# GpSimd and VectorE by turns in the planner, weight scans as squares on ScalarE, v split in two operations, two more second layers in sevens

## The chip, the cores and the metric

One core of one Trainium2 chip. The metric is device time in microseconds (us) for one execution. Engines are named as in the profile: PE is TensorE's matmul and PEld its weight load, DVE is VectorE, ACT is ScalarE, POOL is GpSimd, SP is SyncE, which here issues every DMA.

## What is computed

The reference is block-sparse attention followed by a mixture of four experts that takes all of them for every token:

```
scores_l = scale * q @ k.T            (only |i - j| < 16 kept)
scores_s = scale * q @ max_of_32(k) + log(32)
a = softmax(concat(scores_l, scores_s))
x = a @ concat(v, mean_of_32(v))      -> 3072 tokens x 512
for e in range(4):
    h = relu(x @ w1[e])               (512 -> 1024)
    out += p[:, e:e+1] * (h @ w2[e])  (1024 -> 512)
```

with 4 batches, 8 heads, 768 positions, 64 channels a head; p is `domain_probs` divided by its sum over the experts. Everything comes in and goes out as fp32.

## The kernel before, in words

**Precision.** Each fp32 matmul is done as three matmuls in a narrower type: an operand is split into a high part (a cast, on ACT) and a low part (the difference, on POOL or DVE), and hi x hi, hi x lo and lo x hi are summed in PSUM. For fp16 parts the weights are scaled to use the type's range. The scale of an expert's two matrices comes from `largest` (line 425), a maximum of absolute values on DVE for each 128 x 512 piece of a weight, collected in `wmax`, and from `scales_of_weights` (line 455), which turns the 128 partial maxima through PE, takes their maximum and makes a power of two and its inverse out of it in a chain of small DVE operations. `scan` (line 468) loads one piece (tile `ws`) and calls `largest`; there are 4 experts x 8 pieces x 2 matrices = 64 of them, in the order of experts 2, 3, 1, 0.

**Stages.** The first 768 tokens are done by `plain_units`, two blocks of 384 with experts 0 and 1 in fp32r; the profile's names there are ph, po<-w. Then follow the four pairs of blocks in `PAIRS` (line 1264), each with its list of experts: pair 0 has experts 2 and 3, pair 1 has 3, 2, 1, 0, pair 2 has 0, 1, 2, 3 and pair 3 has 3, 2, 1, 0. For pairs, the first layer (`first`, line 1516) is a 2 x 2 block product with seven instead of eight products (the table `SEVEN`; PSUM tiles pha to phd). The combined operands of x are made once for each pair by `x_operands`, those of w1 once for each expert by `w1_operands` (tiles `w1g`, kept in DRAM and loaded again by later pairs).

**The second layer** has two forms. The plain form is `mm2`, called by `second` and `tile_by_tile` (po<-w2s,h, 512 columns): for each of six tiles of 128 tokens eight slices of the hidden units with three matmuls each. Its weights come from `w2_scaled` (line 1104; tiles `w2s`, stored once and loaded by later pairs), and it is interleaved with the first layer of the next expert. The other form is `second_sevens` (line 1415; poa to pod, 256 columns): the same 2 x 2 scheme with seven products. Its weights come from `w2_operands` (line 1193; tiles `w2g`), which loads two raw pieces, scales them on ACT, makes four casts on ACT, four combinations on DVE and four low parts, one half on POOL and the other on the engine that is passed as `low`. Its hidden units are combined and split by `h_operands` (line 1474). `SEVENS` (line 1265) lists the pairs and experts that use this form: experts 0, 1, 2 of pair 2 and all of pair 3. `fetch7` (line 1297) prepares the next entry of `todo7` during a second layer, `fetch2` the next of `todo2`, which holds the plain ones.

**Attention** runs in between as 64 pieces of 96 queries x 4 heads: `load_piece`, `stage_a` (line 608: splits k, q and v), `scores`, `probs`, `transposed`, `values`, `to_x`. From the second batch on, `stage_a` scales v on ACT, casts it on ACT and subtracts on POOL.

**The order.** No engine call is issued at once. Each becomes a `Step` (line 87) with a cost from a formula for its engine (`takes`, how long the engine is held, and `lasts`, when the result is there). `order_of` (line 164) then runs a list scheduler over the whole program: `forward` (line 298) places ready steps by rank on the five engines, with buffers given out in order of first use; `backward` (line 321) does the same from the end and gives new ranks. Ten rounds are made and the best order kept, and the kernel is issued in that order. The constants stand at lines 65 to 67: `WAIT` (signalling between engines), `SPARE` (a tenth added to the cost of every step on ACT, DVE and POOL) and `ROUNDS`.

## Time and profile before

| | |
|---|---|
| time, median of 3 runs | 1079.7 us (1079.17 to 1083.99) |
| profiled execution | 1079.39 us, span 1077.5 us, mean granted clock 0.995 |
| instructions | 22082 |
| DMA | 194.95 MB, 181 GB/s over the span |
| stages, by the time of their matmuls | plain blocks up to 207 us, pair 0 to about 352, pair 1 to about 606, pair 2 to about 850, pair 3 to the end |

[...] A group of instructions is written out<-in with the tile names above. A wait is listed as who waited, for whose result. "PE 98% busy" counts matmuls from start to modelled end, so the pitch of matmuls in a clean run is the better price.

### The profile page before, as it was taken

How to read it: one execution, taken by the hardware profiler on the slowest of the kernel's cores; microseconds unless marked ns; L12 is line 12 of the kernel's file. 1: busy time of each engine (PE TensorE's matmuls, PEld its weight loads, DVE VectorE, ACT ScalarE, POOL GpSimd, SP SyncE). 2: the span in 40 equal slices, each digit the busy share in tenths (PEclk: the TensorE clock that was granted, in tenths of full speed). 3: DMA queues.
4: the chain of work that ended last, by engine and by line, in shares of the span. 5: the costliest groups of instructions: out<-in, count | busy, mean ns of one | idle time of the engine just before them, and what ended most of it. 6: DMA issues, size and time to landing. Idle time of an engine off the chain costs nothing.

```text
span 1077.5 us, 22082 instructions
## 1 busy us (share of the span) xinstructions
PE 1051.8 (98%) x7497; PEld 707.7 (66%) x7497; DVE 866.0 (80%) x2102; ACT 730.2 (68%) x1992; POOL 607.2 (56%) x716
## 2 busy tenths in 40 slices
PE   9988999899999999999999999999999999999998
PEld 7977888654554555555555568686775567686867
DVE  6898889988877867988988897998767775969473
ACT  5776688887864744976977796988545763748170
POOL 2599588877743211852856887896532352717050
PEclk9999999989999999999999999999999999999999
DMA  8789887987888889789676664657422440424001
GB/s 287 212 202 244 227 220 198 274 270 198 240 245 253 253 232 254 220 268 263 207 231 170 167 176 126 176 163 217 116 83 89 135 149 16 162 66 151 1 15 59
DMA packets 172897, 194.95 MB, mean 181 GB/s; under 512 B 80368, under 2 KB 117232, under 8 KB 172784
## 3 DMA queue, kind: packets, MB, share of 16 engines
q1 hardware_dynamic: 172784, 193.55, 62.3%
q8 instruction: 58, 0.95, 0.4%
q14 instruction: 55, 0.45, 0.1%
HBM read 141.33 MB, written 35.65 MB: 164 GB/s over the span
## 4 chain that ended last, share of the span: by engine, by line
PE 66%; DVE 5%; POOL 2%; ACT 2%; DMA 1%; issue 1%; SPq 0%; DVEq 0%; POOLq 0%; ACTq 0%
PE po L373 16%; PE phb L373 13%; PE pha L373 8%; PE pob L373 7%; PE poa L373 5%; PE phd L373 4%; PE phc L373 4%; PE poc L373 3%; PE pod L373 2%; PE psc L373 2%; PE px L373 1%; POOL w2g L373 1%; DVE wr L373 1%; DMA wr<-in_w2L 1%; ACT ms L373 0%
## 5 line engine op out<-in xcount | busy, mean ns | idle before, releaser
L373 PEld LDWEIGHTS <-w1g 128*128 128x128 f16 x2352 | 229.2, 98 | 174.2 <-issue 13.0
L373 PEld LDWEIGHTS <-h 128*128 128x128 f16 x1764 | 171.0, 98 | 115.9 <-issue 0.5
L373 PE MATMUL po<-w2s,h 128*128 128x512 f16 x1008 | 239.6, 379 | 0.0
L373 PE MATMUL phb<-x_t,w1g 128*128 128x384 f16 x1008 | 195.3, 327 | 4.6 <-DVE phc L373 1.9
L373 POOL TENSOR_TENSOR w2g<-wr,w2g 128x512 f16<-128x512 f32 (+1 forms) x80 | 90.1, 1133 | 114.3 <-ACT w2g L373 112.1
L373 PE MATMUL pha<-x,w1g 128*128 128x384 f16 x672 | 133.3, 329 | 2.9 <-DVE nb L373 2.9
L373 ACT ACTIVATE ms<-ms,nb 96x152 f32<-96x152 f32 x256 | 104.0, 414 | 15.5 <-DVE nb L373 15.2
L373 PEld LDWEIGHTS <-hs 128*128 128x128 f16 x1008 | 98.0, 98 | 12.7 <-issue 0.4
L373 POOL TENSOR_TENSOR v<-qv,v 128x256 f16<-128x256 f32 (+1 forms) x56 | 45.7, 816 | 104.6 <-ACT v L373 89.7
L373 DVE CUSTOM_DVE_ANT_0 ms<-psc,c_sb 96x152 f32<-96x152 f32 x256 | 69.1, 305 | 31.3 <-PE psc L373 30.5
L373 POOL TENSOR_TENSOR h<-r,h 128x384 f16<-128x384 f32 x56 | 57.1, 1025 | 54.1 <-ACT h L373 51.5
L373 ACT CAST w2g<-wr 128x512 f16<-128x512 f32 (+1 forms) x112 | 61.6, 562 | 32.2 <-DVE wr L373 18.7
L373 POOL TENSOR_TENSOR w<-wr,w 128x512 fp32r<-128x512 f32 x48 | 65.3, 1368 | 26.2 <-ACT w L373 20.3
L373 DVE TENSOR_TENSOR aw<-ms,aw 96x512 f16<-96x512 f32 (+1 forms) x104 | 69.7, 686 | 6.3 <-ACT aw L373 6.3
L373 PE MATMUL ph<-xh,w 128*128 128x384 f32 x256 | 69.4, 343 | 5.1 <-ACT w L373 3.6
L373 PE MATMUL phd<-x_t,w1g 128*128 128x384 f16 x336 | 65.6, 326 | 2.6 <-POOL w1g L373 1.7
L373 PE MATMUL phc<-x,w1g 128*128 128x384 f16 x336 | 66.1, 326 | 0.0
L373 PE MATMUL poa<-w2g,h 128*128 128x256 f16 x504 | 65.4, 273 | 0.4 <-DVE nb L373 0.4
L373 PE MATMUL pob<-w2g,hs 128*128 128x256 f16 x504 | 64.0, 273 | 0.3 <-DVE poc L373 0.3
L373 POOL TENSOR_TENSOR ks<-kr,ks 128x304 fp32r<-128x304 f32 x56 | 53.3, 952 | 16.3 <-ACT ks L373 15.7
L373 PE MATMUL po<-w,hh 128*128 128x512 f32 x192 | 60.8, 396 | 0.0
L373 ACT ACTIVATE wr<-wr,scalew 128x512 f32<-128x512 f32 x72 | 51.8, 719 | 11.2 <-DMA wr<-in_w2L 7.7
(195 smaller groups left out, 2350.1 us busy)
## 6 DMA issues: line engine op xcount, KB each, us to landing
wr<-in_w2L SPq DMA_DIRECT2D x112, 256.0 KB, 3.3
w1g<-wdg SPq DMA_DIRECT2D x34, 512.0 KB, 4.1
w1g<-wdg SPq DMA_DIRECT2D x34, 384.0 KB, 3.8
ws<-in_w1L SPq DMA_DIRECT2D x32, 256.0 KB, 3.8
ws<-in_w2L SPq DMA_DIRECT2D x32, 256.0 KB, 3.8
wx<-in_w1L SPq DMA_DIRECT2D x32, 256.0 KB, 4.7
wdg<-w1g SPq DMA_DIRECT2D x16, 512.0 KB, 4.5
wd<-w2s SPq DMA_DIRECT2D x16, 512.0 KB, 5.1
```

What stands on the lines that cost most here:

```text
L373: program.append(Step(self.key, lambda: getattr(self.engine, name)(*a, **kw), name, a, kw))
```

## The change

- The planner's costs for ACT, DVE and POOL are given anew, with `SPARE` 0. A `Step` has a mark `port`: all of POOL's, and those of DVE that work on SBUF alone (with two tensors, or one-tensor copies and scalar operations of more than one column). In `forward` and `backward` two steps with that mark follow each other, less 135 ns (`HOLD`).
- The ten rounds become 13 entries of `SEARCH`: each adds noise to the ranks in a stretch of the program and then makes some passes; the last order is used.
- `largest` becomes a square with a sum over the columns, on ACT; the square root is taken in `scales_of_weights` as a logarithm and an exponential with scale 0.5, and the tops of the ranges are changed to match. A scan's step may not start before 37 us of the planner's time (`floor`).
- `stage_a` makes v's parts with an ACT multiplication straight into the high part and one DVE operation for the low part.
- `SEVENS` gets experts 3 and 2 of pair 1, and the low parts of their weights go to POOL.

```diff
+HOLD = 135.0
+SPARE, SPARE_DMA, LANES = 0.0, 300.0, 8
+SEARCH = ((0, 0, 0, 0, 13), (118596, 76, -926166, -909577, 4), ...
...
+        self.port = key == "POOL" or key == "DVE" and self.shares(op)
...
+    def shares(self, op):
+        inside = all(x.space != bass.MemoryType.PSUM for x in (*self.written, *self.read))
+        if op in ("tensor_tensor", "scalar_tensor_tensor"):
+            return inside
+        return inside and op in ("tensor_scalar", "tensor_scalar_mul", "tensor_scalar_add", "tensor_copy") and self.moved() > 1
...
         if op == "activation" and "accum_out" in kw:
-            return 420.0 * (1 + SPARE), 560.0 + 420.0 * SPARE
+            t = 420.0 if n < 200 else 175.0 + 0.85 * n
+            return t * (1 + SPARE), t * (1 + SPARE) + 140.0
...
-        elif op in ("tensor_tensor", "scalar_tensor_tensor"):
-            t = 260.0 + 1.1 * n if n > 8 else 180.0
+        elif op == "tensor_tensor":
+            t = 62.0 + 1.055 * n
+        elif op == "scalar_tensor_tensor":
+            t = 120.0 + 1.055 * n
...
                 else:
+                    if s.port:
+                        t = max(t, port - HOLD)
+                        port = t + s.lasts
                     end[n] = t + s.lasts
...
-    best = None
-    for _ in range(ROUNDS):
-        order, start, end = forward(rank)
-        if best is None or max(end) < best[0]:
-            best = max(end), order
-        rank = backward(start, end)
-    return best[1]
+    for seed, spread, lo, hi, passes in SEARCH:
+        noise = random.Random(seed).gauss
+        rank = [r + noise(0.0, spread) if lo < r < hi else r for r in rank]
+        for _ in range(passes):
+            order, start, end = forward(rank)
+            rank = backward(start, end)
+    return order
...
-    X_TOP, W1_TOP = 4.0, 0.25
+    X_TOP, W1_TOP, W2_TOP, ROUND = 4.0, 1.0, 4.0, 1.0 + 2.0**-8
...
     def largest(e, fc, which, raw):
-        V.tensor_reduce(
-            wmax[:, e, which, fc : fc + 1], raw, axis=AX.X, op=ALU.max, apply_absolute_value=True
-        )
+        A.activation(raw, raw, AF.Square, scale=ROUND, accum_out=wmax[:, e, which, fc : fc + 1])
...
         V.tensor_reduce(m, wmax[:, e], axis=AX.X, op=ALU.max)
+        V.tensor_scalar_max(m, m, 2.0**-120)
+        A.activation(m, m, AF.Ln)
+        A.activation(m, m, AF.Exp, scale=0.5)
         s, back = scales(f"w{e}", m, 2)
...
         largest(e, fc, which, raw)
+        program[-1].floor = 37e3
...
         if b:
-            A.mul(vr, vr, scale_v[b])
-            A.copy(v12[:, :, 0, :], vr)
-            PL.tensor_tensor(v12[:, :, 1, :], vr, v12[:, :, 0, :], op=ALU.subtract)
+            A.mul(v12[:, :, 0, :], vr, scale_v[b])
+            V.scalar_tensor_tensor(v12[:, :, 1, :], vr, scale_v[b], v12[:, :, 0, :], op0=ALU.mult, op1=ALU.subtract)
...
-    SEVENS = {(pr, e) for pr, es in PAIRS[2:] for e in (es if pr == 3 else es[:3])}
+    IN_SEVENS = {0: 0, 1: 2, 2: 3, 3: 4}
+    SEVENS = {(pr, e) for pr, es in PAIRS for e in es[: IN_SEVENS[pr]]}
...
-            w2_operands(e, i, *(("chunk", CHUNKS) if i == 3 and pr == 3 and e != es_of[3][0] else ("x", NX)), PL if pr == 2 else V)
+            w2_operands(e, i, *(("chunk", CHUNKS) if i == 3 and pr == 3 and e != es_of[3][0] else ("x", NX)), PL if pr < 3 else V)
```

## Rows read from the trace of the kernel before

**Rows 1.** The page's part 1: busy us (share of the span) and instructions, each engine.
```profile
PE 1051.8 (98%) x7497; PEld 707.7 (66%) x7497; DVE 866.0 (80%) x2102; ACT 730.2 (68%) x1992; POOL 607.2 (56%) x716
```
**Rows 2.** Busy us (instructions) by stretch; then granted clock, DMA share, GB/s.
```profile
37.00:205.00 168.00, 161.63 (x1115) 137.56 (x1114) 149.58 (x397) 127.28 (x380) 138.57 (x151) 1.00 0.86 230
205.00:250.00 45.00, 36.43 (x226) 21.37 (x225) 41.17 (x97) 38.25 (x108) 34.43 (x46) 0.89 0.82 252
250.00:352.00 102.00, 100.30 (x656) 52.24 (x654) 83.56 (x226) 70.23 (x214) 60.72 (x81) 1.00 0.83 237
352.00:510.00 158.00, 157.87 (x1057) 87.27 (x1055) 124.89 (x325) 101.87 (x292) 56.58 (x81) 1.00 0.86 249
510.00:630.00 120.00, 119.32 (x771) 63.61 (x770) 103.26 (x262) 96.74 (x276) 89.23 (x104) 1.00 0.67 191
...
675.00:702.00 27.00, 27.00 (x203) 16.77 (x201) 25.36 (x59) 25.27 (x70) 23.59 (x26) 1.00 0.67 188
```
**Rows 3.** Waits of PE, 37 to 205 us: us in total, times, longest us.
```profile
PE ph L373 <- ACT w L373: 3.6, 3, 1.6
```
**Rows 4.** Timeline of DVE at 217 us: start us, us, instruction.
```profile
217.55 2.09 DVE L373 TENSOR_TENSOR aw<-ms,aw 96x96 f16<-96x96 f32 x1
```
**Rows 5.** Timeline of PE, 207 to 210 us; in brackets the idle time before.
```profile
207.44 0.50 PE L373 MATMUL phd<-x_t,w1g 128*128 128x384 f16 x2
209.63 0.66 PE L373 MATMUL phd<-x_t,w1g 128*128 128x384 f16 x3 [1.70 <-POOL w1g L373]
```
**Rows 6.** Busy us in the stretch of 216 to 222 us, columns as in rows 2.
```profile
216.00:222.00 6.00, 4.79 (x16) 2.27 (x16) 6.00 (x16) 3.87 (x14) 4.33 (x6) 0.50 0.95 256
```
**Rows 7.** Clean runs of matmuls in the chain that ended last: start us, us.
```profile
821.46 30.43 PE po L373 x141
...
1053.04 1.31 PE poc L373 x12
```
**Rows 8.** Groups by shape: busy us, mean ns of one, idle us before and its releasers.
```profile
L373 POOL TENSOR_TENSOR w2g<-wr,w2g 128x512 f16<-128x512 f32 x52 | 67.0, 1292 | 82.7 <-ACT w2g L373 81.2 <-DVE wr L373 1.5
L373 ACT ACTIVATE wr<-wr,scalew 128x512 f32<-128x512 f32 x72 | 51.8, 719 | 11.2 <-DMA wr<-in_w2L 7.7 <-DVE scalew L373 2.5 <-POOL w2g L373 1.0
L373 ACT CAST w2g<-wr 128x512 f16<-128x512 f32 x84 | 50.6, 615 | 31.7 <-DVE wr L373 18.7 <-PE poc L373 11.6 <-PE po L373 1.0
L373 DVE TENSOR_REDUCE wmax<-ws 128x1 f32<-128x512 f32 x64 | 42.6, 673 | 0.6 <-DMA ws<-in_w2L 0.6
L373 ACT ACTIVATION_READ_ACCUMULATOR ms<-ms,nb 96x1 f32 x224 | 42.4, 189 | 0.0
L373 POOL TENSOR_TENSOR v<-qv,v 128x256 f16<-128x256 f32 x48 | 39.2, 817 | 104.6 <-ACT v L373 89.7 <-DMA awT<-aw 13.6 <-DMA ws<-in_w1L 1.3
L373 DVE TENSOR_TENSOR wr<-wr,wr 128x256 f32<-128x256 f32 x56 | 36.6, 659 | 2.0 <-POOL w2g L373 1.1 <-ACT wr L373 0.4
L373 DVE TENSOR_TENSOR aw<-ms,aw 96x96 f16<-96x96 f32 x48 | 26.1, 544 | 1.7 <-ACT aw L373 1.7
L373 ACT CAST v<-qv 128x256 f16<-128x256 f32 x48 | 19.3, 401 | 13.9 <-PE px L373 13.6
L373 DVE SCALAR_TENSOR_TENSOR w2s<-wr,scalew,w2s 128x512 f16<-128x512 f32 x16 | 13.9, 868 | 0.0
...
L373 ACT ACT_TABLE_LOAD x1 | 1.3, 1283 | 0.7 <-PEq L1716 0.7
```
**Rows 9.** Busy us of the scans (tile wmax) by stretch: DVE, clock, DMA, GB/s.
```profile
37.00:205.00 168.00, 12.24 (x19) 1.00 0.86 230
205.00:250.00 45.00, 5.46 (x9) 0.89 0.82 252
352.00:510.00 158.00, 18.11 (x29) 1.00 0.86 249
```
**Rows 10.** Timeline of the first pair expert's factor: its turn through PE and its end.
```profile
159.37 0.27 PE L373 MATMUL pmw<-c_sb,wm 128*2 128x128 f32 x1
...
200.83 0.15 DVE L373 TENSOR_SCALAR one<-scalew 128x1 f32<-128x1 f32 x1
```

More of the change, by code (lines that the diff above doesn't have):

```diff
@@ L2 @@
 import math
+import random
 from contextlib import ExitStack
@@ L65 @@
 WAIT = dict(PE=53, ACT=33, DVE=33, POOL=76, SP=28)
-SPARE, SPARE_DMA, LANES = 0.1, 300.0, 8
-ROUNDS = 10
+HOLD = 135.0
+SPARE, SPARE_DMA, LANES = 0.0, 300.0, 8
+SEARCH = ((0, 0, 0, 0, 13), (118596, 76, -926166, -909577, 4), (780266, 614, -235174, -212853, 4), (329500, 1477, -899917, -889859, 3), (76061, 51, -483011, -417535, 3), (321819, 442, -325437, -253148, 3), (65853, 4887, -736259, -698405, 2), (915255, 52, -732600, -614407, 4), (3082, 1198, -904408, -886754, 3), (634517, 146, -972159, -939192, 1), (610557, 63, -1200000, 0, 4), (577881, 63, -805892, -733694, 1), (710128, 877, -584763, -530364, 3))
 def columns(ap):
@@ L101, in __init__ @@
         self.takes, self.lasts = getattr(self, key)(op, kw)
-        self.behind, self.ahead, self.tiles, self.glued = {}, [], [], False
+        self.port = key == "POOL" or key == "DVE" and self.shares(op)
+        self.behind, self.ahead, self.tiles, self.glued, self.floor = {}, [], [], False, 0.0
     def moved(self):
@@ L137, in DVE @@
             t = 75.0 + 1.04 * n + 55.0 * any(columns(x) == 1 for x in self.read)
-        elif op in ("tensor_tensor", "scalar_tensor_tensor"):
-            t = 260.0 + 1.1 * n if n > 8 else 180.0
-        elif op in ("tensor_scalar", "tensor_scalar_mul") and n < 10:
-            t = 300.0
+        elif op == "tensor_tensor":
+            t = 62.0 + 1.055 * n
+        elif op == "scalar_tensor_tensor":
+            t = 120.0 + 1.055 * n
+        elif op != "tensor_reduce" and op != "reciprocal":
+            t = 85.0 + (1.055 if n < 50 else 0.55) * n
         else:
@@ L147, in POOL @@
         n = self.moved()
-        t = 250.0 + 2.1 * n if op == "tensor_tensor" else 100.0 + 1.5 * n
-        return t * (1 + SPARE), t * (1 + SPARE) + 10.0
+        if op == "tensor_tensor":
+            t = 165.0 + (1.9 if BYTES[self.written[0].dtype] == 2 else 2.1) * n
+        else:
+            t = 130.0 + (1.5 if n < 100 else 0.96) * n
+        return t * (1 + SPARE), t * (1 + SPARE) + 25.0
     def SP(self, op, kw):
@@ L235, in order_of, with __init__ @@
     class Run:
-        def __init__(self, rank, queue, count):
+        def __init__(self, rank, queue, count, floor):
             self.rank, self.queue = rank, queue
@@ L242, in __init__ @@
                 self.left[head[n]] += count[n] + len(steps[n].tiles)
-            self.ready = [0.0] * len(steps)
+            self.ready = list(floor)
             self.uses = {name: len(at) for name, at in uses_of.items()}
@@ L298, in forward @@
     def forward(rank):
-        run = Run(rank, queue, [sum(head[m] != head[n] for m in steps[n].behind) for n in every])
+        run = Run(rank, queue, [sum(head[m] != head[n] for m in steps[n].behind) for n in every], [s.floor for s in steps])
         run.after_slot = lambda n: WAIT[keys[n]]
+        port = 0.0
         lanes, wire, order = [0.0] * LANES, 0.0, []
@@ L321, in backward @@
     def backward(start, end):
-        lasts = [end[n] - start[n] for n in every]
+        lasts = [s.lasts if s.port else end[n] - start[n] for n, s in enumerate(steps)]
         takes = [s.takes for s in steps]
@@ L335, in backward @@
             count,
+            [0.0] * len(steps),
         )
@@ L338, in backward @@
         run.begin()
-        rank, done = [0.0] * len(steps), 0
+        rank, done, port = [0.0] * len(steps), 0, 0.0
         while done < len(steps):
@@ L342, in backward @@
             for n in reversed(group):
+                if steps[n].port:
+                    t = max(t, port + lasts[n] - takes[n])
+                    port = t + takes[n] - HOLD
                 for m, lag in back[n]:
@@ L457, in scales_of_weights @@
         V.tensor_reduce(m, wmax[:, e], axis=AX.X, op=ALU.max)
+        V.tensor_scalar_max(m, m, 2.0**-120)
+        A.activation(m, m, AF.Ln)
+        A.activation(m, m, AF.Exp, scale=0.5)
         s, back = scales(f"w{e}", m, 2)
-        one = const.tile([P, 2], F32, name=f"one{e}")
+        one = const.tile([P, 3], F32, name=f"one{e}")
         V.tensor_scalar_mul(one[:, 0:1], s[:, 0:1], W1_TOP)
+        V.tensor_scalar_mul(one[:, 2:3], s[:, 1:2], W2_TOP)
         V.scalar_tensor_tensor(
-            one[:, 1:2], back[:, 0:1], 1.0 / (X_TOP * W1_TOP), back[:, 1:2], op0=ALU.mult, op1=ALU.mult
+            one[:, 1:2], back[:, 0:1], 1.0 / (X_TOP * W1_TOP * W2_TOP), back[:, 1:2], op0=ALU.mult, op1=ALU.mult
         )
-        scale_w[e], back_w[e] = (one[:, 0:1], s[:, 1:2]), one[:, 1:2]
+        scale_w[e], back_w[e] = (one[:, 0:1], one[:, 2:3]), one[:, 1:2]
     scans = [(e, fc, which) for e in (2, 3, 1, 0) for fc in range(FC) for which in range(2)]
```

2 lines of the change are left out of this document (1 added, 1 removed).

## The prediction

> **What bounds the kernel now.** I read the page's engine line first, then busy time by stretch, then what TensorE waited for, then the timeline of the one stretch where it stood still. The engine line [rows 1] shows TensorE busy 98% of 1077.5 us: this is a TensorE kernel, and only two things can shorten it, fewer matmuls or less standing still. The table by stretch [rows 2] says where it stands still. From 250 us on it is busy almost without a gap (100.30 of 102, 157.87 of 158, 119.32 of 120). From 37 to 205 us it lacks 168 - 161.63 = 6.4 us, and from 205 to 250 us 45 - 36.43 = 8.6 us, at a mean granted clock of 0.89, which costs another 0.11 x 45 = 5.0 us. So 205 to 250 us loses 13.6 us, and 37 to 250 us loses 20.0 of the run.
>
> What stands in the way there? Before 205 us the largest single wait of a matmul is for ScalarE's cast of a weight [rows 3]. After 205 us VectorE is the late one: it is busy 41.17 of 45 us [rows 2], it runs nine weight scans there, 5.46 us [rows 9], in the same queue as the operands TensorE needs, and one of its operations on SBUF alone takes 2.09 us [rows 4] where the mean of its kind is 0.544 [rows 8]: its time is mostly a wait, and GpSimd was working beside it. [...]
>
> **The change, part by part.**
>
> *Sevens.* Second layer of the second pair, experts 3 and 2. Each now takes 6 tiles x 8 slices x 3 = 144 matmuls of 512 columns; in sevens 3 tiles x 7 products x 4 x 3 = 252 of 256 columns. A clean run of the first is 30.43 / 141 = 0.2158 us each, of the second 1.31 / 12 = 0.1092 us [rows 7]. 31.08 - 27.51 = 3.57 us for each expert, **7.1 us** for two, all on the path, since TensorE has no gap there.
>
> What it costs elsewhere. Eight calls of `w2_operands`: ScalarE 2 x 0.719 + 0.401 + 3 x 0.615 = 3.68 us, GpSimd 0.817 + 3 x 1.292 = 4.69 us, VectorE 4 x 0.65 = 2.6 us each [rows 8]; together 29.4, 37.5 and 20.8 us. The hidden units are combined as well: for each of 8 chunks ScalarE makes five more casts of 384 columns (0.51, between 0.401 and 0.615), GpSimd five more subtractions (about 1.05, between 0.817 and 1.292), VectorE two more operations on SBUF (0.99, from 0.659 at 256): 20.4, 42 and 15.8 us. Evictions: 12 more ScalarE copies of 256 columns (4.8 us); VectorE 18 operations of 256 columns for six of 512, at 0.434 and 0.868 some 5.2 us. SP's queue loses the four loads of the second expert's stored parts (512 KB) and gains 16 raw ones of 256 KB: 12 issues and 2 MB more, 8.4 us at the 249 GB/s of that stretch, where the DMA engines are busy 0.86 of the time [rows 2]. I cost that at nothing, because the loads have the stretch from 250 us to hide in; without that cover it is up to 8 us.
>
> *Scans.* 64 reductions of 0.673 us, 43.1 us, leave VectorE [rows 8]. ScalarE gets 64 squares with a sum. None is in the trace. Nearest rows: a 512-column cast, 0.615, and the read of the accumulator behind each exponential, 0.189 [rows 8]; 0.615 if the read hides, 0.804 if not. I take 0.615, the operation's own row: 39.4 us, with 51.5 as the other end.
>
> *Logarithm and exponential* in `scales_of_weights`, once for each expert, plus two small VectorE operations. The logarithm is a function that ScalarE doesn't use yet, and the trace holds one table load, 1.283 us [rows 8]. Lower bound no further load; upper bound two for each expert, one to the logarithm's table and one back, 8 x 1.283 = 10.3 us of ScalarE. I take eight, and 1.5 us of it on TensorE's path: each load blocks only what stands behind it on ScalarE, and TensorE runs on from other PSUM banks. The path's own bounds are 0 and 10.3. The planner doesn't know these loads. [...]
>
> *v in two operations.* 48 times a GpSimd subtraction (0.817) and a ScalarE cast (0.401) go, 39.2 and 19.2 us; 48 VectorE operations come, 256 columns wide, nearest row 0.868 at 512 [rows 8], so half of it, 0.434 (20.8 us), up to 0.868 if it waits for GpSimd.
>
> *The planner* now lets GpSimd and VectorE work on SBUF by turns, has tighter costs and disturbs its ranks. It adds no work. What it can win is the standing still, 20.0 us of it between 37 and 250 us; it can lose too, because the order it writes has no spare left (SPARE 0.1 to 0).
>
> **Loads after.** ScalarE 730 + 39.4 + 29.4 + 20.4 + 4.8 - 19.2 + 10.3 + 2 = 817 us (76%), GpSimd 607 + 37.5 + 42 - 39.2 = 647 (60%), VectorE 866 - 43.1 + 20.8 + 20.8 + 15.8 + 5.2 = 885 (82%). By stage, 37 to 250 us: VectorE 190.8 - 17.7 for its 28 scans [rows 9] + about 5 = 178 of 213 (from 90 to 84%), GpSimd 173 - 8 = 165, ScalarE 165.5 + 32 x 0.615 - 4 + 4 x 1.283 + 1 = 187 (from 78 to 88%). From 352 to 510 us ScalarE would have 101.9 + 20.4 + 4.8 + 14.7 + 29 x 0.615 - 4 + 5.1 = 161 of 158 us, with the 29 scans that stand there [rows 9], if nothing moved. So scans and preparations must move into 250 to 352 us (70.23 of 102 busy) or behind 510; over 250 to 630 us it is 268.8 + 69 = 338 of 380, 89%. That such a load can be carried is in the trace: from 675 to 702 us ScalarE is busy 25.27 and VectorE 25.36 of 27 us, and TensorE misses nothing [rows 2].
>
> **The sum.** The profiled execution took 1079.39 us (span 1077.5 and 1.9 around it), 0.3 us under the median of 1079.7. Less 7.1 (sevens). Less 9 of the 13.6 us lost in 205 to 250 us: the nine scans go from the queue that is late, and the waits between GpSimd and VectorE become visible to the planner; the bounds are 0 and 13.6. Less 1 of the 6.4 us before, where ScalarE's casts, which get more company, are what is waited for. Plus 1.5 (tables) and 2.5 (the crowd on ScalarE from 330 to 510 us; bounds 0 and 8, the overflow of 3 us and 29 unhidden reads of 0.189). 1079.39 - 13.1 = 1066.3: **1066 us**. What is late next: ScalarE.
>
> **Rivals.**
> 1. *The early stall goes altogether.* For it: VectorE falls to 84% there and the wait of 2.09 us is of the kind that the planner now sees. Against: ScalarE rises to 88%. 1079.4 - 7.1 - 13.6 - 4 = 1055 us.
> 2. *ScalarE's crowd eats the sevens*, and the model of turns changes little on the chip. For it: 161 of 158 us. Against: the slice at 94%. 7 us back, half of the early gain: 1079.4 - 7.1 - 5 + 9 = 1076 us.
> 3. *Slower: the factor for the first expert of the first pair comes late.* Now its maxima are transposed at 159.37 us and its factor is there at 200.83 [rows 10]; the first matmul that needs it starts at 207.44 [rows 5], 6.6 us later. The links between are short, so rank and queues, not work, make up the 41 us. The change puts a logarithm, an exponential, two table loads and a last scan from a fuller ScalarE into this chain. Beyond 6.6 us each microsecond is one of TensorE, since the plain stage is over by then; above 13 us late the kernel is slower than before. With 15 us and 3 for the clock that falls behind a stall: 1079.4 - 7.1 + 18 = 1090 us. Against: the planner orders exactly such chains, and the scans can start at 37 us.
> 4. *A clean schedule everywhere*: rival 1 with the rest of the 37 to 205 us gap and ends closed gives about 1051 us; it only sets the low end.
>
> **How the numbers follow.** Forecast 0.53, rivals 1 and 4 together 0.20, rival 2 0.16, rival 3 0.11. Half a per cent, 5.4 us either way of 1079.7, is what a measurement of this kernel can tell from no change. Faster (below 1074.3): the forecast and rivals 1 and 4, less the forecast's upper tail: 0.72. Within: rival 2 and that tail, 0.17. Slower: 0.11. The range, 1051 to 1082 us, takes in rivals 1, 2 and 4 and the table loads at their upper bound on the forecast (1066 + 8.8 = 1075) with the crowd's (1080.5); it leaves out most of rival 3.
>
> **What would show it.** TensorE: 504 more matmuls of 256 columns and 288 fewer of 512, no gap beyond about 4 us between 205 and 250 us, no slice at half clock. ScalarE: 64 squares of some 0.6 us, eight further table loads, busy about 817 us; VectorE without 0.673 us reductions of weights. Wrong, if TensorE's waits for ScalarE grow by more than 5 us between 330 and 510 us (rival 2), if it stands still before its first pair's first matmul (rival 3), or if the table loads are none or take longer.

## The result and the profile after

The changed kernel takes 1093.44 us, the median of seven runs (1087.71 to 1100.64), against 1079.7 before: a ratio of 1.0121 with a 95% interval of 1.0100 to 1.0142. It is slower, where the forecast was 1066 us and the range ended at 1082. The profiled execution took 1087.71 us, span 1085.9, which is 8.4 us more than the span before. It is the fastest of the seven, with a mean granted clock of 0.986 where the other six had 0.970 to 0.980: at the median's 0.980 the clock takes 0.006 x 1092 = 6.6 us more by estimate, so the trace below shows less half clock than the kernel usually has, and what the 13.7 us between the medians have over 8.4 goes with that.

The page's part 1 of the changed kernel, engine by engine, answers to [rows 1]:

```profile
PE 1057.7 (97%) x7713; PEld 737.0 (68%) x7713; DVE 896.4 (83%) x2166; ACT 799.7 (74%) x2188; POOL 661.4 (61%) x740
```

The work is what the prediction had worked out: 216 more matmuls, ScalarE at 800 us (817 forecast), VectorE at 896 (885), GpSimd at 661 (647). So the surprise is not in the loads of the engines. The table by stretch, columns as in [rows 2], first of the kernel before for two stretches ahead of those in [rows 2]:

```profile
12.00:31.00 19.00, 18.90 (x171) 16.68 (x171) 16.55 (x78) 13.56 (x39) 6.38 (x16) 1.00 0.71 251
31.00:48.00 17.00, 16.85 (x130) 15.35 (x130) 14.56 (x53) 13.45 (x37) 7.70 (x9) 1.00 0.76 232
```

and of the changed kernel:

```profile
12.00:31.00 19.00, 17.76 (x155) 15.21 (x154) 14.32 (x69) 12.91 (x38) 6.38 (x16) 1.00 0.61 215
31.00:48.00 17.00, 16.17 (x79) 13.66 (x78) 6.19 (x31) 6.94 (x22) 1.43 (x2) 0.50 0.27 76
...
37.00:205.00 168.00, 155.70 (x1027) 131.03 (x1027) 139.63 (x383) 130.87 (x401) 123.19 (x133) 0.95 0.81 213
205.00:250.00 45.00, 42.10 (x282) 30.42 (x279) 35.12 (x94) 41.38 (x120) 31.27 (x36) 0.96 0.93 253
250.00:352.00 102.00, 101.87 (x664) 54.59 (x663) 98.41 (x242) 87.91 (x247) 80.10 (x94) 1.00 0.76 219
352.00:510.00 158.00, 154.36 (x1266) 108.06 (x1264) 141.53 (x359) 144.31 (x413) 115.03 (x127) 0.99 0.87 247
```

The operations that the prediction had to price from neighbours [rows 8], groups by shape of the changed kernel:

```profile
L396 POOL TENSOR_TENSOR w2g<-wr,w2g 128x512 f16<-128x512 f32 x76 | 100.0, 1319 | 102.6 <-ACT w2g L396 102.4
...
L396 ACT ACTIVATE ws<-ws 128x512 f32<-128x512 f32 x64 | 40.2, 628 | 0.0
L396 DVE SCALAR_TENSOR_TENSOR v<-qv,vscale,v 128x256 f16<-128x256 f32 x48 | 28.6, 597 | 0.1
...
L396 ACT ACTIVATION_READ_ACCUMULATOR ws<-ws 128x1 f32 x64 | 12.3, 192 | 0.0
L396 ACT ACT_TABLE_LOAD x9 | 11.5, 1283 | 0.9 <-PEq L1742 0.7
```

A square takes 0.628 us (0.615 taken; the read behind it mostly hides, since the next operation starts 0.624 us after the square in the median), v's second part 0.597 on VectorE (0.434 taken, 0.868 the other end), and there are eight table loads beside the first, as taken.

In the table by stretch two things stand out. The stall of 205 to 250 us, where the prediction expected its gain, did shrink: busy 42.10 of 45 us where it was 36.43, and the clock 0.96 where it was 0.89. But from 31 to 48 us TensorE runs at a granted clock of 0.50 and finishes 79 matmuls where it finished 130. A busy share of 16.17 of 17 us hides this: it is 0.205 us for each matmul, where 16.85 us for 130 were 0.130.

Busy time can't price that, so the rest of this section and the experiments use one more quantity, worked out from the trace. Take every matmul's time from its start to the next one's start (the 12 score or value matmuls of a piece as one block). The lower quartile of these, for matmuls of the same tiles and width over the two traces, is the clean pitch; what a pitch is longer than that is TensorE's **loss**, standing still and half clock together. Work without loss is the sum of the clean pitches. In us, by stretch, with the time at half clock in the last column (the end of the run left out):

```
                     work   0-31  31-48 48-205 205-250 250-352 352-510 510-end  loss   half
before             1026.6    2.7    0.8   14.2   13.4    3.5    2.1    9.0    45.8    10.2
after              1019.3    4.5    8.8   25.0    5.6    1.6    7.8    8.1    61.3    30.7
e1_scores_first    1019.3    4.1    1.1   27.4    5.2    1.7    7.8    7.6    54.9    20.5
e2_one_table       1019.3   10.3   10.0   23.9    5.1    1.9    3.2    8.4    62.8    44.4
e3_both            1019.3    2.5    1.2   25.1    1.0    1.6    3.0    8.4    42.8    10.2
b1_sevens          1019.3    6.0    0.9   19.9   11.9    9.5   13.3   15.4    77.0    20.5
b2_squares         1026.6    3.2    3.5   18.9   11.4    2.2    1.6   10.2    51.0    20.5
b3_planner         1026.6   10.3    8.5   23.9    9.9    3.1    1.6    7.6    65.0    58.0
b4_planner_first   1026.6    2.3    1.3   23.2    7.5    3.4    1.7    8.2    47.5    13.7
b5_no_planner      1020.7    3.1    5.1   19.1   10.7    1.0   20.7   12.6    72.3    30.7
e4_dve_scans       1019.3    2.8    0.9   17.0   21.9    3.2    8.1    9.0    62.8    27.3
e5_no_sevens       1026.6    2.6    1.1   26.6    1.2    1.5    1.6   10.7    45.4    17.1
e6_short_squares   1019.3    4.2    0.8   27.3    1.1    1.4    3.1    7.6    45.5    17.1
e7_no_turns        1019.3    2.7    1.1   30.7   10.2    4.8   23.7   69.4   142.8    44.4
e9_one_start       1019.3    1.8    1.1   14.6   15.6    2.9    5.7    6.2    48.0    17.1
e10_copy_low       1019.3    3.9    1.1   22.1    0.8    2.1    3.0    7.5    40.6    17.1
```

The first two lines are the result. The work fell by 7.3 us, the sevens as forecast (7.1). The loss rose by 15.5: 9.8 before 48 us, 10.8 from 48 to 205, 5.7 from 352 to 510, against 7.8 gained from 205 to 250 and 2.8 in the rest. 15.5 - 7.3 = 8.2, the 8.4 of the spans (the rest is rounding and the end of the run). The lines below are the experiments.

What TensorE waits for in the changed kernel, whole run (us in total, times, longest us):

```profile
PE pmw L396 <- ACT wm L396: 5.6, 2, 3.0
PE ph L396 <- POOL w L396: 5.1, 5, 1.8
PE ph L396 <- ACT w L396: 4.2, 4, 1.9
PE psc L396 <- DVE nb L396: 2.1, 5, 0.4
...
PE pmw L396 <- DVE dgw L396: 1.2, 1, 1.2
```

Three kinds: pmw, the transposition of an expert's maxima, for the logarithm and exponential on ScalarE; psc, scores, for the VectorE maximum; ph, the plain first layer, for the two halves of a weight. Only the last was in the list of before, with 3.6 us for ScalarE's half [rows 3]. The other two can be followed to their cause in the timelines.

*psc.* TensorE and VectorE of the changed kernel near 29 us (start us, us, instruction, idle time before and its releaser):

```profile
28.88 0.44 PE L396 MATMUL psc<-k,qv 64*96 64x128 f32 x2
29.73 0.34 PE L396 MATMUL psc<-ksr,qv 64*96 64x24 f32 x2 [0.41 <-DVE nb L396]
```
```profile
29.35 0.31 DVE L396 CUSTOM_DVE_ANT_0 ms<-psc,c_sb 96x152 f32<-96x152 f32 x1
29.59 0.08 DVE L396 DVE_READ_ACCUMULATOR2_ANT nb<- 96x1 f32 x1
30.11 0.31 DVE L396 CUSTOM_DVE_ANT_0 ms<-psc,c_sb 96x152 f32<-96x152 f32 x1 [0.44 <-PE psc L396]
```

One PSUM tile takes two heads: four score matmuls, then two maxima. On each engine these instructions stand in the same order as before, but in the one list in which the new planner issues the instructions, VectorE's maximum of the first head now stands ahead of the second head's matmul. Where the list has it so, the program gets a wait of the matmul on the maximum, although the two touch different columns. So TensorE stands 0.41 us, and VectorE then stands 0.44 us for TensorE. Three such waits lie between 12 and 31 us; 1.4 us behind the last one, at 31.1 us, the clock falls. In the kernel before, TensorE has no wait for the maximum there.

*pmw.* ScalarE, then TensorE, of the changed kernel near 244 us:

```profile
242.97 1.28 ACT L396 ACT_TABLE_LOAD   x1
244.26 0.20 ACT L396 ACTIVATE wm<-wm 128x2 f32<-128x2 f32 x1
244.37 0.39 ACT L396 CAST w1g<-wx 128x256 f16<-128x256 f32 x1
244.78 1.28 ACT L396 ACT_TABLE_LOAD   x1
246.07 0.20 ACT L396 ACTIVATE wm<-wm 128x2 f32<-128x2 f32 x1
```
```profile
243.03 0.66 PE L396 MATMUL phb<-x_t,w1g 128*128 128x384 f16 x3
246.33 0.37 PE L396 MATMUL pmw<-c_sb,wm 128*2 128x128 f32 x1 [2.63 <-ACT wm L396]
```

The logarithm and the exponential each bring a table load of their own, 1.28 us, with 0.01 us between the load and the function; eight in the run beside the first. TensorE stood for 2.63 us and started none of the matmuls that stand behind the transposition in its order before the transposition itself at 246.33; the next, into phb, started at 246.50. At 246.2 us the clock falls for 3.4 us more.

### The profile page after: what moved, and what is told of

It is laid out like the page before. It is cut to its first block, busy times and chain, and to the rows that moved or that the text cites. A ratio compares the mean times of both kernels' runs of the same rounds, so it can differ in the third digit from the quotient of the medians.

```text
span 1085.9 us, 22860 instructions
## 1 busy us (share of the span) xinstructions
PE 1057.7 (97%) x7713; PEld 737.0 (68%) x7713; DVE 896.4 (83%) x2166; ACT 799.7 (74%) x2188; POOL 661.4 (61%) x740
## 4 chain that ended last, share of the span: by engine, by line
PE 82%; ACT 5%; DVE 5%; POOL 3%; issue 2%; DMA 2%; SPq 1%; POOLq 0%; DVEq 0%; ACTq 0%
PE po L396 18%; PE phb L396 13%; PE pob L396 10%; PE pha L396 9%; PE poa L396 7%; PE phd L396 4%; PE phc L396 4%; PE psc L396 4%; PE pod L396 3%; PE poc L396 3%; PE ph L396 3%; PE px L396 2%; PE pav L396 1%; POOL w L396 1%; ACT ms L396 1%
## 5 line engine op out<-in xcount | busy, mean ns | idle before, releaser
L396 PEld LDWEIGHTS <-h 128*128 128x128 f16 x1692 | 163.6, 98 | 91.0 <-POOL h L396 0.5
L396 POOL TENSOR_TENSOR w2g<-wr,w2g 128x512 f16<-128x512 f32 (+1 forms) x112 | 127.3, 1144 | 152.0 <-ACT w2g L396 147.6
L396 PE MATMUL po<-w2s,h 128*128 128x512 f16 x720 | 168.1, 379 | 0.0
L396 PEld LDWEIGHTS <-hs 128*128 128x128 f16 x1296 | 126.4, 98 | 17.7 <-issue 0.9
L396 ACT CAST w2g<-wr 128x512 f16<-128x512 f32 (+1 forms) x144 | 78.7, 563 | 47.7 <-DVE wr L396 32.4
L396 POOL TENSOR_TENSOR h<-r,h 128x384 f16<-128x384 f32 x72 | 72.0, 1010 | 62.1 <-ACT h L396 56.2
L396 PE MATMUL poa<-w2g,h 128*128 128x256 f16 x648 | 86.9, 273 | 0.0
L396 POOL TENSOR_TENSOR w<-wr,w 128x512 fp32r<-128x512 f32 x48 | 67.3, 1409 | 30.6 <-ACT w L396 21.3
L396 PE MATMUL pob<-w2g,hs 128*128 128x256 f16 x648 | 84.5, 273 | 0.8 <-DVE poc L396 0.6
L396 ACT ACTIVATE wr<-wr,one 128x512 f32<-128x512 f32 x88 | 62.7, 720 | 9.0 <-DMA wr<-in_w2L 8.7
L396 POOL TENSOR_TENSOR hs<-s,hs 128x384 f16<-128x384 f32 x52 | 54.6, 1059 | 11.2 <-ACT hs L396 11.1
```

The source lines that it names most:

```text
L396: program.append(Step(self.key, lambda: getattr(self.engine, name)(*a, **kw), name, a, kw))
```

## The experiments

**The changed kernel again, and the two causes taken away.** The first run has no edit.

> The changed kernel once more, nothing edited, beside the kernels that follow. Theory A (the loss is built into the order: waits of score matmuls on DVE before 31 us, table loads ahead of four scale factors, late operands between 48 and 205 us): again 1087 to 1100 us, with TensorE at half clock from about 31 us on for 10 us or more, and four stalls of 2 to 6 us at the transposition of wm. Rival B (a matter of the chip that the first runs had): within 5 us of 1079.7, with no half clock before 200 us.

Measured: 1092.7 us, ratio 1.0080 [1.0045, 1.0115]. The waits and the fall of the clock (33.2 to 50.3 us) are there again: theory A. Of its four stalls at the transposition of wm two are there, 2.64 and 3.00 us; a third, 1.25 us, is for VectorE.

The second edit changes the issued list alone; every engine keeps its order:

```diff
     for n in order:
+        while not gone.issuperset(needs.get(n, ())):
+            ...
+            issue(queue.pop(0))
         if n not in gone:
             issue(n)
```

Here `needs` names, for a maximum, the four score matmuls of its tile, and `queue` is TensorE's own order.

> The changed kernel with one edit to the list that is issued: a DVE maximum of the first-tokens stage is issued only behind all four score matmuls that fill its PSUM tile; the order on each engine stays what it was. It takes away the waits of score matmuls on the DVE maximum (three stalls of 0.4 us between 12 and 31 us on TensorE, with DVE idle behind them). Theory A (these waits make TensorE late by 2 us, that gap brings the half clock at 31 us, and that one the rest): no half clock at 31 us, loss of TensorE before 48 us down from 13.3 to about 4 us, time 8 to 10 us less than the changed kernel's on this chip, about 1084. Rival B (the half clock at 31 us has another cause, the work that stands there is simply thinner): the half clock stays and the time is within 2 us of the changed kernel's. Rival C (the time saved is lost again, as the scan loads and splits behind set the pace): no half clock, but under 4 us less.

Measured: 1080.52 us, 0.9978 [0.9961, 0.9995], 12.2 us less than the changed kernel beside it. The two stretches of e1_scores_first, columns as above:

```profile
12.00:31.00 19.00, 19.00 (x168) 16.65 (x167) 14.39 (x70) 13.69 (x40) 6.40 (x16) 1.00 0.63 214
31.00:48.00 17.00, 16.62 (x135) 15.01 (x134) 11.99 (x47) 13.38 (x38) 6.49 (x8) 1.00 0.55 163
```

No gap from 12 to 31 us, no half clock in the stretch behind, 135 matmuls instead of 79. Theory A, and more than its 8 to 10 us; B and C fall. The two profiled spans differ by 7.8 us; what the medians have over that goes mostly with the granted clock of the other executions, 0.980 to 0.984 in the changed kernel and 0.989 to 0.994 in this one. A few waits of 0.4 us cost 12.

The third takes the table loads away with one instruction:

```diff
+    nc.scalar.preload_act_table_set("natural_log_exp_and_others")
     c_sb = const.tile([P, C_N], F32, name="c_sb")
```

> The changed kernel with one instruction in front: ScalarE loads, before its first work, the one table set that holds Exp and Ln, so that no later function needs another. 9 table loads become 1; nothing else is touched. Theory A (the eight loads stand in the chain of four scale factors and TensorE waits in order behind the transposition of wm): the waits of pmw on ACT wm (5.6 us and 6.2 us of the profile) shrink to under half, the fall of the clock at 246 and 505 us goes, time 5 to 8 us less than the changed kernel's. Rival B (the chain is late because of its DVE steps and the squares in ScalarE's queue, the loads lie in idle time): under 2.5 us less, TensorE waits on DVE or on the last square in its place.

Measured: 1079.93 us, 0.9979 [0.9962, 0.9997], 12.8 us less than the changed kernel. The group of table loads of e2_one_table:

```profile
L431 ACT ACT_TABLE_LOAD x1 | 1.3, 1283 | 0.7 <-PEq L1743 0.7
```

Of the waits for wm 0.2 us are left, and the loss from 352 to 510 us falls from 7.8 to 3.2. That is theory A, at nearly twice its price. Its profiled execution was the longest of its eleven (1089.21 us, with 41 us at half clock behind the psc waits, which this kernel keeps), so its lines before 100 us say nothing about the tables.

The fourth has both edits.

> The two edits together: maxima behind their four score matmuls, and one table set for the whole run. Theory A (the two causes lie in different stretches, 12 to 48 us and 160 to 505 us, and add): 13 to 18 us less than the changed kernel, 1075 to 1080, level with the kernel before or a few us under it; what is left over the plan is the loss between 48 and 205 us. Rival C (what one stretch gives, the next one takes back, since scans and splits have their own pace): under 10 us less, over 1083.

Measured: 1069.87 us (1068.84 to 1070.87), 0.9875 [0.9849, 0.9901]: 22.8 us less than the changed kernel and faster than the kernel before. This is the best kernel of the study with the whole computation. Stretches of e3_both, and what is left of the wait for wm:

```profile
205.00:250.00 45.00, 44.93 (x303) 29.87 (x303) 40.65 (x106) 42.68 (x124) 33.26 (x42) 1.00 0.88 240
250.00:352.00 102.00, 101.93 (x683) 53.64 (x682) 98.05 (x243) 87.15 (x254) 83.86 (x97) 1.00 0.85 242
352.00:510.00 158.00, 157.28 (x1288) 111.26 (x1287) 146.16 (x360) 144.51 (x415) 115.19 (x130) 1.00 0.88 245
```
```profile
PE pmw L396 <- ACT wm L396: 0.2, 1, 0.2
```

From 205 us on TensorE hardly stops. The two causes add, theory A: 22.8 us where 12.2 and 12.8 make 25.0 and 13 to 18 were expected. What remains is the loss from 48 to 205 us, 25.1 us, 10.9 more than before.

**The parts alone, in the kernel before.** Sevens for the second pair's first two experts:

```diff
-    SEVENS = {(pr, e) for pr, es in PAIRS[2:] for e in (es if pr == 3 else es[:3])}
+    IN_SEVENS = {0: 0, 1: 2, 2: 3, 3: 4}
+    SEVENS = {(pr, e) for pr, es in PAIRS for e in es[: IN_SEVENS[pr]]}
```

> The kernel before with one part of the change: the second pair's first two experts in seven products, GpSimd subtracting their low halves. Planned again by the planner of before. Theory A (the term of the prediction): TensorE's work without waits falls by 7.3 us, and 6 to 8 us of it reach the end, about 0.993 of the kernel before. Rival B (the extra splits crowd ScalarE and GpSimd between 352 and 510 us): under 3 us, with new waits of TensorE on w2g or on the second pair's h parts in that stretch. Rival C (the planner's order changes elsewhere): the gain in 352 to 510 us is there but another stretch loses as much.

Measured: 1099.31 us, 1.0180 [1.0155, 1.0205]. The work falls by the 7.3 us, and the loss rises by 31: none of the theories expected it on this scale, C comes nearest. Stretches of b1_sevens:

```profile
250.00:352.00 102.00, 96.20 (x619) 50.75 (x620) 93.62 (x228) 77.68 (x218) 72.45 (x90) 0.98 0.83 239
352.00:510.00 158.00, 151.18 (x1210) 104.38 (x1208) 142.83 (x353) 120.04 (x336) 108.82 (x125) 0.98 0.75 213
```

Where the kernel before missed 1.7 and 0.1 us, this one misses 5.8 and 6.8, with waits in 250 to 510 us of 3.1 us for x_t from ScalarE and of 2.9 and 2.8 us in all for nb and xs from VectorE. VectorE has the scans and the sevens' combinations, 142.83 of 158 us. Fewer matmuls alone make this kernel slower.

The squares alone, with one table set, so without the loads:

```diff
-        V.tensor_reduce(wmax[...], raw, axis=AX.X, op=ALU.max, apply_absolute_value=True)
+        A.activation(raw, raw, AF.Square, scale=ROUND, accum_out=wmax[...])
```

> The kernel before with another part alone: all scans of the weights as squares on ScalarE with Ln and Exp behind them, the planner's price for such a square at 610 ns, and one table set loaded first, so that no later load of a table is in it. No least start for the squares. Theory A (the prediction's term: DVE in 205 to 250 us is what TensorE waits for, and the squares free it): loss of TensorE in 205 to 250 us falls from 13.4 to under 6 us, time 6 to 10 us less. Rival B (the stall is moved, not removed: ScalarE's splits of the plain weights come later behind the squares): loss in 205 to 250 us falls, loss in 48 to 205 us rises from 14 to over 20 us, time within 3 us of before.

Measured: 1087.3 us, 1.0048 [1.0026, 1.0069]. Loss from 205 to 250 us 11.4 (13.4 before), from 48 to 205 us 18.9 (14.2). Rival B in its direction, short of its 20 us: the stall moves to earlier work, and this kernel is even slower. It also has one wait of a score matmul for the maximum, 0.41 us at 32.1 us, and 6.8 us of half clock from 34.6 us on, although the planner is the one of before.

The new planner alone, with the work of the kernel before:

```diff
-SPARE, SPARE_DMA, LANES = 0.1, 300.0, 8
-ROUNDS = 10
+HOLD = 135.0
+SPARE, SPARE_DMA, LANES = 0.0, 300.0, 8
+SEARCH = ((0, 0, 0, 0, 13), ...
...
```

> The work of the kernel before, every instruction of it, in an order made by the changed kernel's planner (new costs, GpSimd and DVE in turns, the list of random starts). Theory A (the late score matmuls before 31 us come from the new planner's list): they are there, TensorE at half clock near 31 us, time 5 to 12 us above before. Rival B (they come with the rest of the change, the new planner by itself is the better one): no half clock there, time 0 to 8 us under before. Loss in 48 to 205 us tells in both cases whether the 11 us more there are the planner's (over 20 us here) or the squares' (under 16 us).

Measured: 1096.5 us, 1.0147 [1.0111, 1.0184], theory A and above its time. From 48 to 205 us it loses 23.9 us with the work of before, so by the test written there the 11 us more of the changed kernel are the planner's order. And the same with the maxima behind their score matmuls:

> The work of the kernel before in the new planner's order, with the maxima issued behind their four score matmuls. To be set beside b3_planner (1.0147), which has the waits. Theory A (the early waits and the half clock behind them are all that was bad in the new planner's order): 10 to 16 us less than b3_planner, 0.995 to 1.003 of before, no half clock before 90 us. Rival B (its order of the plain stage is worse too): loss in 48 to 205 us still over 20 us, 1.004 or more.

Measured: 1080.81 us, 0.9985 [0.9964, 1.0005], 1.6% less. The stretch of 31 to 48 us of b3_planner and of b4_planner_first:

```profile
31.00:48.00 17.00, 16.59 (x81) 14.07 (x79) 7.99 (x34) 6.65 (x19) 2.02 (x5) 0.50 0.21 63
```
```profile
31.00:48.00 17.00, 16.68 (x128) 15.17 (x127) 14.70 (x51) 12.65 (x35) 6.08 (x9) 1.00 0.70 221
```

Theory A of both: the new planner's list has the early waits with the work of before too, and taking them away gives back all it lost (one fall of the clock, 3.4 us at 59.9 us, is left before 90 us). They aren't the new planner's alone: b2_squares and b5_no_planner, ordered by the old one, have one each, at 32.1 us. Rival B of the second has its condition met as well (23.2 us lost from 48 to 205 us), but not its time, since 205 to 250 us loses 5.9 less.

Everything but the planner:

> The kernel before with everything of the change but its planner: squares, Ln and Exp with one table set, v in two operations, sevens. Planned by the planner of before, with the new price of a square. Theory A (each part needs the other: the squares free DVE for the sevens): sevens alone cost 1.8% and squares alone 0.5%, together 0.985 to 0.995. Rival B (what makes the sum come out is the planner, since the extra splits have to be laid beside others): 1.0 to 1.015, with loss in 250 to 450 us over 8 us.

Measured: 1098.56 us, 1.0157 [1.0131, 1.0183]. Loss from 352 to 510 us 20.7 us; its longest wait there is one of phd for x_t from ScalarE, 6.3 us. Rival B, slightly above its time: with the planner of before the crowd that the prediction saw on ScalarE does stand in TensorE's way.

**One part less, in e3_both.** The scans back on VectorE (the diff of b2_squares turned round):

> The changed kernel with maxima behind their four score matmuls, and with the scans back on DVE as absolute maxima (so no Ln, no Exp of factors and one table set in any case); planner, v, and sevens as changed. To be set beside e3_both. Theory A (the squares relieve DVE in 205 to 250 us): 4 to 10 us slower than e3_both's 0.9875, loss in 205 to 250 us over 8 us. Rival B (the new planner hides the scans on DVE as well, and squares on ScalarE cost the plain stage what they give later): within 3 us of e3_both, loss in 48 to 205 us down from 25 to under 18 us.

Measured: 1090.17 us, 1.0099 [1.0071, 1.0128], 2.3% over e3_both, planned again with the same list of starts. Loss from 205 to 250 us 21.9, from 48 to 205 us 17.0. Theory A, at double its price; and half of rival B is true, because the earlier stretch loses 8 us less.

The sevens undone (`IN_SEVENS = {0: 0, 1: 0, 2: 3, 3: 4}`):

> The kernel of e3_both with the second pair's first two experts back in eight products. Theory A (the prediction's term of 7.3 us is met in full once the rest is in place): 6 to 9 us slower than e3_both, loss of TensorE between 250 and 510 us the same within 2 us. Rival B (the crowd on ScalarE between 352 and 510 us eats part of it): 2 to 5 us slower.

Measured: 1080.43 us, 1.0000 [0.9984, 1.0015], 1.3% over e3_both. Theory A, 10.6 us by the medians where it had 6 to 9. The profiled spans differ by 9.7 us, 7.3 of work and 2.6 of loss, and the loss from 250 to 510 us is 3.1 against 4.6: with the rest in place the sevens are met in full. The 2.6 can be the order, since this kernel was planned again with the same list of starts.

**What sets the loss from 48 to 205 us.** Squares cut to an eighth, in the same order:

```diff
+        program[-1].issue = lambda: nc.scalar.activation(
+            raw[:, 0:64], raw[:, 0:64], AF.Square, scale=ROUND, accum_out=wmax[:, e, which, fc : fc + 1]
+        )
```

> The kernel of e3_both in the same order on every engine, each square over 64 columns of 512 only, so the weights' factors come from an eighth of the elements. A square then takes some 0.2 us instead of 0.62. Theory A (the squares in ScalarE's queue make the casts of the plain weights late between 48 and 205 us): loss of TensorE there falls from 25 us to under 19, time 4 to 9 us less than e3_both. Rival B (there GpSimd's subtractions of w, 94% busy from 48 to 100 us, and the loads set the pace): loss there within 2 us, time within 3 us.

Measured: 1068.75 us, 0.9876 [0.9848, 0.9904]. A square took 0.254 us instead of 0.629, and the loss there is 27.3 us, not less. Rival B: their length is not it.

The rule of turns left out of the planner:

```diff
-        self.port = key == "POOL" or key == "DVE" and self.shares(op)
+        self.port = False
```

> The kernel of e3_both, planned without the rule that GpSimd's operations and DVE's operations inside SBUF take turns; costs, random starts and work as there. Theory A (the rule describes the chip, so that an order made without it slips): 4 us or more slower than e3_both, with the loss spread over the stretches in which both engines are busy. Rival B (the rule holds the plan back for nothing): within 2 us of e3_both or faster, loss in 48 to 205 us below 25 us.

Measured: 1167.92 us, 1.0805 [1.0781, 1.0829]. Theory A, but far beyond it; the loss is above all behind 510 us. The longest wait in total of e7_no_turns, and its stretch of 850 to 1060 us, then the same stretch of e3_both:

```profile
PE phb L396 <- DVE phc L396: 26.1, 26, 2.4
```
```profile
850.00:1060.00 210.00, 195.86 (x1342) 130.75 (x1340) 143.80 (x267) 112.26 (x247) 72.68 (x77) 0.99 0.31 96
```
```profile
850.00:1060.00 210.00, 209.78 (x1610) 157.23 (x1609) 144.23 (x263) 109.74 (x245) 80.17 (x80) 1.00 0.25 79
```

VectorE is busy as long in both, so it is not short of time; its operations come in an order that makes TensorE wait for phc again and again. The list of starts is that of the planner with the rule on; an order with other starts and no rule wasn't tried, so the 8% are the price of this order, not of the rule in general.

Every second low part of the plain w2 on VectorE:

```diff
-                w2[fc] = weights(w2L, e, fc, "2", PL)
+                w2[fc] = weights(w2L, e, fc, "2", V if fc % 2 else PL)
```

> The kernel of e3_both with every second low part of the plain w2 subtracted by DVE instead of GpSimd, planned again. Theory A (GpSimd's subtractions of 1.29 us, one behind the other, set the loss in the plain stage): loss in 48 to 205 us falls from 25 to under 18 us, time 3 us or more less than e3_both. Rival B (the ring of queues is as tight on DVE): the loss there stays within 4 us of 25, time within 3 us of e3_both or slower.

Measured: 1071.06 us, the median of three (the fourth took 2729.71 us), 0.9918 [0.9892, 0.9943], 0.4% over e3_both: rival B by its time. Its loss by stretch isn't known, since the fourth is the one that was profiled.

The first entry of the list of starts alone (`SEARCH = ((0, 0, 0, 0, 13),)`):

> The kernel of e3_both, planned from the first entry of the list of starts alone (13 passes, no random change of ranks). Theory A (the random starts found an order that holds on the chip): 4 to 10 us slower than e3_both. Rival B (the random starts bought time in the plan that the chip does not give): within 3 us of e3_both.

Measured: 1075.72 us, 0.9955 [0.9938, 0.9971], 0.8% over e3_both. Theory A. Its loss is 14.6 us from 48 to 205 us and 15.6 from 205 to 250, together 30.2; e3_both has 26.1, the kernel before 27.6.

At last GpSimd's low parts of the plain weights made short, in the same order:

```diff
+        if lo_engine is PL:
+            program[-1].issue = lambda: nc.gpsimd.tensor_copy(lo, raw)
```

> The kernel of e3_both in the same order on every engine; the low part of a plain weight is a copy on GpSimd instead of a subtraction (so the plain experts are computed with a wrong low part). 48 operations of 1.43 us become some 0.6 us. Theory A (GpSimd's time, and the DVE operations that go slower beside it, set the loss before 250 us): loss of TensorE between 48 and 250 us falls from 26 to under 16 us, time 8 us or more less than e3_both. Rival B (ScalarE's queue and the order set it): loss there still over 22 us, time within 4 us of e3_both.

Measured: 1060.88 us (1058.81 to 1066.96), 0.9796 [0.9762, 0.9830]. The low parts took 0.736 us instead of 1.427. The stretch of 48 to 250 us of e3_both, then of e10_copy_low:

```profile
48.00:250.00 202.00, 190.79 (x1269) 152.03 (x1269) 177.04 (x471) 167.08 (x512) 156.61 (x172) 0.97 0.87 227
```
```profile
48.00:250.00 202.00, 193.77 (x1288) 156.28 (x1287) 162.97 (x478) 169.93 (x521) 122.34 (x175) 0.97 0.88 232
```

This one is split. By the medians 9 us are gone, which is theory A. But the profiled execution, the longest of its four, lost 22.9 us there, which is rival B: GpSimd has 34 us less to do and VectorE 14, TensorE no longer waits for GpSimd's half of a weight, and waits 7.2 us for ScalarE's cast of it instead. The granted clock tells the two apart. The profiled execution has 13.7 us at half clock in this stretch, e3_both 10.2; less half of that, as an estimate, what is left of the loss fell from 21.0 to 16.1 us. The other three executions had a clock of 0.997 to 0.999 against 0.992 in the profiled one, by estimate worth 5 to 7 us of the 5 to 8 they are faster. So GpSimd's time is a part of it, behind it stands ScalarE's queue, and most of the rest is fewer falls of the clock; why those executions had fewer stays open.

## Why the prediction was wrong

**Sevens, -7.1: right.** The work fell by 7.3 us, and e5_no_sevens shows the whole of it on the path. What was not said is the condition: b1_sevens loses 31 us with the same sevens. The prediction costed the work they bring to the other engines with 2.5 us of a crowd on ScalarE and nothing for the loads; that holds only with VectorE freed of the scans and with an order that spreads the splits.

**The planner, "adds no work, what it can win is the standing still": the step that failed most.** The sum had no term for a loss by the planner, and the tables by stretch began at 37 us. Before 48 us the loss rose by 9.8 us, and e1_scores_first gives 12.2 us back by the issued list alone. The prediction looked at what the planner does to the order on the engines and not at what else hangs on its list: the waits that the program gets. The rest of the planner was undervalued: b5_no_planner against e3_both is 2.9%.

**Tables, +1.5: mis-sized.** Eight loads were taken and eight came, of 1.28 us, and e1_scores_first to e3_both, which differ by them alone, is 10.7 us, about the upper bound of 10.3 and not 1.5. The argument that failed is that each load blocks only what stands behind it on ScalarE. TensorE's transposition waits for ScalarE, and all of TensorE behind it: 5.6 + 1.2 us of waits, and two falls of the clock of 3.4 us each behind them (at 240 and 500 us in e1_scores_first) that e3_both doesn't have. Half clock counted as half lost, that is 6.8 + 3.4 = 10.2 us by estimate; that it also comes to eight loads' time looks like chance. On ScalarE itself the trace shows no cost beyond the load: it begins at 242.97 and the next function at 244.26, 1.29 us later, and ScalarE was idle for 0.9 us in all ahead of the nine loads. With the set `natural_log_exp_and_others` loaded first e2_one_table has a single load, so none of the eight was needed; but the set did not come by itself.

**205 to 250 us, -9, and 37 to 205 us, -1: the stall was moved, not removed.** From 205 to 250 us 7.8 us were gained, 12.4 in e3_both. But from 48 to 205 us 10.8 and 10.9 us were lost in its place, and 9.7 in b3_planner with the work of before, so by the planner's order. The two together are 27.6 us before, 30.6 after and 26.1 in e3_both; in b2_squares, b4_planner_first, e6_short_squares and e9_one_start they are 28 to 31. The prediction took the two stretches for two limits. By these sums they look like one stage, with one amount of preparation for it on three engines, and the order mostly chooses where TensorE pays for it; this is argued from the sums. That amount does count, as e4_dve_scans (38.9 us with the scans on VectorE) and e10_copy_low (22.9) show, and an order can also pay more, as e7_no_turns (40.9).

**The crowd on ScalarE, +2.5: the right engine, and carried.** ScalarE was busy 144.31 of 158 us, and in e3_both the loss there is 0.9 us over that of before. b5_no_planner shows the other case, 20.7 us.

**Rivals.** Rival 3 had the right sign and the right chain, logarithm, exponential and tables ahead of a factor, but the wrong place: the first pair's factor was ready at 186 us, 15 us sooner than in [rows 10], and the price was paid at the transpositions of the later experts, through TensorE's order. Its 3 us for a clock that falls behind a stall were the author's estimate: the kernel before has 10.2 us at 0.50 there, 6 of them in [rows 6], and the changed one 3.4 us from 246.2 us on, behind the stall of 2.63 us; half of that lost, by estimate, is 5.1 and 1.7 us. Rivals 1, 2 and 4 had the stall of 205 to 250 us shrink as well, and none a price for it before 205 us. Without the two causes e3_both comes to 0.9875 of before, and the forecast was 0.9873; that this agrees is in part chance, since in it 12.4 us gained stand against 10.9 lost where 9 and 1 gained were written.

## What to carry to other kernels

A planner writes more than an order for each engine: where waits are derived from the issued list, two instructions on different engines that touch one tile should stand in the order in which the tile is used, here all matmuls of a PSUM tile ahead of its first reader. A function that is new to an engine is priced by what waits for it in order, on the engine behind as well, and the table set is chosen once at the start: with one load in place of nine e2_one_table took 12.8 us less. And before a stall is counted as gone, ask what the stretches ahead of it still have to do: its loss may only change its place.

## What the runs showed of the hardware that was not expected

*Short gaps and the clock.* In the changed kernel three stalls of 0.41 us, at 16.9, 25.1 and 29.7 us, were followed by 17.1 us at 0.50. In the profiled execution of e2_one_table a single such stall, at 19.8 us, was followed by 41.0 us, from 21 us on (b3_planner, with TensorE busy 18.59 of the 19 us from 12 to 31, has a clock of 0.68 there and of 0.50 from 31 to 48):

```profile
19.75 0.34 PE L396 MATMUL psc<-ksr,qv 64*96 64x24 f32 x2 [0.41 <-DVE nb L396]
```
```profile
21.00:31.00 10.00, 10.00 (x50) 8.77 (x50) 4.55 (x21) 3.83 (x12) 2.08 (x6) 0.50 0.38 110
```

In e1_scores_first, with TensorE busy 19.00 of 19 us, the clock was 1.00 from 12 to 48 us. Not every short stall is followed by a fall: after the first two of the changed kernel none came for at least 6 us, and e3_both, where TensorE lacks 0.38 of the 17 us from 31 to 48, has a clock of 1.00 there. While the clock was at 0.50, VectorE and ScalarE of the changed kernel were busy 6.19 and 6.94 of 17 us, where those of the kernel before had been busy 14.56 and 13.45: the engines that feed on TensorE did about half as much in that stretch.

*VectorE beside GpSimd.* In the trace of e3_both, the median time of an operation on VectorE that lay beside a busy GpSimd for under 5% of its time, or for over half of it:

```
operation of VectorE                        alone    beside
wr<-wr, 128x256, two inputs in SBUF         0.415    0.763 us
w1g<-wx,w1g, 128x256, two inputs in SBUF    0.412    0.626 us
rs<-rs, 96x4, TENSOR_SCALAR inside SBUF     0.155    0.440 us
phc<-phb,p, one input in PSUM               0.554    0.553 us
ms<-psc,c_sb, one input in PSUM             0.307    0.303 us
```

and for the scans, one input in SBUF, 0.674 and 0.673 us in the trace of before. So in these rows both operations with two inputs in SBUF took longer beside GpSimd, by 0.35 and 0.21 us, and so did this scalar operation with one, by 0.29; those with an input in PSUM and the scans took the same within 0.004 us. That is the line which the planner's rule of turns draws. It isn't as sharp everywhere: v's second part in the changed kernel, with two inputs in SBUF, took 0.474 us alone and 0.478 beside in the median, though up to 1.378 beside.
